# One order of the same operations exchanged for another: 2757 places, 425 PSUM banks and the engines of shared operations

## The chip, the core and the metric

The kernel runs on one core of a Trainium2 chip. The core has five instruction streams: TensorE (PE, with its weight loads PEld), VectorE (DVE), ScalarE (ACT), GpSimd (POOL) and SyncE (SP), which here only issues DMAs. Each works through its own list in order, and they meet through semaphores. The metric is device time in microseconds of one execution.

## The reference, cut to what matters

```python
# attention: batch 8, heads 8, seq 576, head_dim 64; block-causal mask, blocks of 64
scores = np.where(mask, scale * np.matmul(q, k.transpose(0, 1, 3, 2)), -1e9)
attn = np.exp(scores - np.max(scores, axis=-1, keepdims=True))
attn = attn / (np.sum(attn, axis=-1, keepdims=True) + 1e-09)
x = np.matmul(attn, v)            # then (8, 576, 512): heads side by side
# mixer, for each of the 8 batches
theta = x @ w_theta
zr, zi = x * np.cos(theta), x * np.sin(theta)
y = np.einsum('ts,bsd->btd', w_tok_r, zr) + np.einsum('ts,bsd->btd', w_tok_i, zi)
u = x + y
return u + np.maximum(u @ w_ch, 0.0)
```

All inputs and outputs are float32.

## The kernel before, in words

There are 64 heads (8 batches of 8). They go in 32 pairs; pair p works on heads 2p and 2p+1, and heads 8b to 8b+7 belong to batch b. A pair's scores are made on PE (L600, L612, with mask rows at L605), their row maxima on DVE (L630, L638), and the exponentials on ACT (L642) into the tiles `t`. The first four pairs turn these on PE (L654) and copy them out (L661, L663). All later ones split `t` into a high and a low float16 part `p` (high on ACT or DVE, L327 or L331; low on DVE, L669), and SP turns the parts with transposing DMAs into `pt`. PE multiplies `pt` with the parts of v (L689, "weighted"), DVE normalises into `x_ring` (L699 to L709), and POOL moves a 64-row piece (L715).

The mixer of batch b needs all its eight heads. `x_ring` is split into high and low parts `xp` (high on ACT or DVE, L325 or L331; low on DVE or POOL, L775), turned by DMA into `xt`; PE makes theta (L789); ACT and DVE make the fraction of a turn (L799, L805) and ACT the sines (L823, L825); the products with x (L835) and their high and low parts `zh` (L325, L329, L331) and `zl` (L848) are shared between DVE, POOL and ACT. PE sums over the sequence ("mix", L858). `u` starts as the sum of the parts of x (L863, DVE or POOL), is scaled (L327, L329, L331), takes the mix (L871), is split into `uhl` (L327 or L331, and L882), multiplied with w_ch on PE (L891), rectified and added (L897), scaled ("fin", L327, L329 or L331) and stored.

The weights are split in the same way at the start: L416 (ACT), L423 and L425 (DVE), L429 (ACT), and L436 (DVE) for the low parts such as `wch_l`.

Nothing sets the order but tables. The function `order_of` (L221) sorts the 2757 steps by the numbers in `PLACES`; each step emits its instructions in that order, so `PLACES` sets the order on every engine and on SP's queue. `BANKS` names the PSUM bank of each accumulation in turn. `ON` names, for each kind of shared operation, the engine of each instance: D for DVE, A for ACT, P for POOL. `RUNNING` (L192) lists fill matmuls, read at L1108 to L1114: an entry (n, bank, count) puts `count` matmuls of a tile of ones, whose result nobody reads, ahead of step n.

Of the kernel before, what the change touches and what calls it, by code (L numbers as in the profile page):

```python
# [189 lines left out]


RUNNING = [  # L192
    (8, 0, 3), (13, 4, 4), (37, 7, 23), (53, 2, 5), (359, 5, 5)
]
ON = {"w5": "DAADDADAD",
      "wc": "DDPPPPDDD",
      "vc": "PDDPDPPPPDPPDPPDDPPDDPPP",
      "qh": "PPPPPPPDPPAAPAADPAADAPADAAPADDAP",
      "vf": "PPDPPPPP",
      "cp": "DDDADAADAADDAAAAAAAAAAAAAAAAAAAA",  # L200
# [966 lines left out]
```

## Time and profile before

| what | us |
|---|---|
| median of 3 runs (661.02 to 663.47) | 663.03 |
| the profiled execution, its own time | 661.59 |
| its span in the profile | 659.8 |
| PE busy in the span | 643.2 |
| DVE busy | 580.5 |
| ACT busy | 466.7 |
| POOL busy | 328.2 |

The span runs from the first instruction to the last; 1.8 us of the execution's time lie around it. A PE matmul is pipelined: a row of 128x288 lasts 287 ns, but the next one starts 122 ns later, so a busy PE may still wait. To see who limits whom one asks, in each stretch, which engine has hardly any idle time, and how much work each engine has left.

### The profile page before, as it was taken

To read this page: it belongs to the slowest core of one execution; us is meant where nothing else is said; L and a number is where in the kernel's file an instruction comes from. 1 tells how busy PE (TensorE), PEld (TensorE's weight loads), DVE (VectorE), ACT (ScalarE), POOL (GpSimd) and SP (SyncE) were. 2 spreads that over 40 slices of the span, in tenths; PEclk is the share of its full clock that TensorE was granted. 3 is DMA by queue.
4 is the path that set the end of the run, shared out by engine and by line. 5 is a ranking of instruction groups with operands and counts; after the bars stand their busy time and mean duration, and the time that the engine had idled before them with its cause. 6 is when DMAs were issued, how large, how long until landed. Compare 5 with 4: busy or idle time off the path is not lost.

```text
span 659.8 us, 17344 instructions
## 1 busy us (share of the span) xinstructions
PE 643.2 (97%) x7153; PEld 504.0 (76%) x7153; DVE 580.5 (88%) x900; ACT 466.7 (71%) x719; POOL 328.2 (50%) x345
## 2 busy tenths in 40 slices
PE   8999989999999999999999999999999999999997
PEld 4899767887678767787787868887787867885775
DVE  4899999989999999999998998999879999754724
ACT  4997897775997788665984679678885887516411
POOL 2310357545528737585256466554574346552800
PEclk9999989999999999999999999999999999999999
DMA  8972288999999799699687879899678887740021
GB/s 308 352 254 77 47 205 145 201 221 180 229 199 182 175 190 192 144 202 177 158 201 187 150 177 183 185 210 240 120 175 160 139 192 131 113 114 19 1 90 73
DMA packets 247647, 110.51 MB, mean 167 GB/s; under 512 B 229008, under 2 KB 229008, under 8 KB 247568
## 3 DMA queue, kind: packets, MB, share of 16 engines
q1 hardware_dynamic: 247568, 109.41, 75.3%
q8 instruction: 56, 0.92, 0.6%
q14 instruction: 23, 0.19, 0.1%
HBM read 43.06 MB, written 9.44 MB: 80 GB/s over the span
## 4 chain that ended last, share of the span: by engine, by line
PE 68%; DVE 21%; ACT 5%; issue 4%; DMA 1%; POOL 0%; DVEq 0%; ACTq 0%; POOLq 0%
PE ps L858 25%; PE ps L891 10%; PE ps L689 10%; PE ps L789 10%; PE ps L600 9%; DVE m L638 5%; DVE p L669 3%; DVE v L586 2%; ACT t L642 1%; ACT p L327 1%; PE ps L654 1%; DVE zl L848 1%; PE ps L1113 1%; DVE u L897 1%; DVE wT_l L436 1%
## 5 line engine op out<-in xcount | busy, mean ns | idle before, releaser
L642 ACT ACTIVATE t<-ps,m 128x192 f32<-128x192 f32 (+4 forms) x288 | 140.8, 555 | 58.8 <-DVE m L638 40.2
L858 PE MATMUL ps<-wT_h,zl 128*128 128x288 f16 x540 | 155.0, 287 | 2.5 <-DVE zl L848 2.5
L858 PE MATMUL ps<-wT_h,zh 128*128 128x288 f16 x540 | 155.4, 288 | 0.7 <-ACT t L642 0.7
L858 PE MATMUL ps<-wT_l,zh 128*128 128x288 f16 x540 | 154.9, 287 | 0.0
L638 DVE TENSOR_REDUCE m<-ps 128x2 f32<-128x640 f32 (+3 forms) x128 | 117.4, 946 | 12.0 <-PE ps L605 11.5
L858 PEld LDWEIGHTS <-zh 128*128 128x128 f16 x1080 | 106.1, 98 | 27.8 <-issue 1.1
L689 PE MATMUL ps<-v,pt 128*128 128x65 f16 (+2 forms) x2668 | 113.3, 201 | 3.8 <-DVE x_ring L706 2.5
L669 DVE SCALAR_TENSOR_TENSOR p<-t,p 128x1664 f16<-128x1664 f32 x56 | 111.8, 2002 | 2.6 <-ACT p L327 2.5
L891 PE MATMUL ps<-uhl,wch_h 128*128 128x288 f16 x512 | 95.4, 286 | 1.1 <-DVE u L897 1.0
L689 PEld LDWEIGHTS <-pt 128*128 128x128 f16 x2436 | 81.5, 97 | 8.8 <-issue 5.5
L789 PE MATMUL ps<-wth_h,xt 128*128 128x512 f16 (+1 forms) x384 | 87.3, 345 | 0.3 <-DVE u L871 0.3
L789 PEld LDWEIGHTS <-xt 128*128 128x128 f16 (+1 forms) x576 | 46.4, 102 | 43.7 <-issue 2.4
L327 ACT ACTIVATE p<-t 128x1664 f16<-128x1664 f32 x46 | 73.3, 1599 | 3.7 <-DMA pt<-p 3.4
L891 PE MATMUL ps<-uhl,wch_l 128*128 128x288 f16 x256 | 73.2, 286 | 0.0
L858 PEld LDWEIGHTS <-zl 128*128 128x128 f16 x540 | 53.1, 98 | 16.3 <-DVE zl L848 3.2
L715 POOL COPY x_ring<-x_ring 64x64 f32<-64x64 f32 x64 | 37.9, 592 | 49.8 <-DVE x_ring L709 22.0
L891 PEld LDWEIGHTS <-wch_h 128*128 128x128 f16 x512 | 48.6, 98 | 14.8 <-issue 2.2
L789 PE MATMUL ps<-wth_l,xt 128*128 128x512 f16 (+1 forms) x192 | 57.3, 344 | 0.0
L835 POOL TENSOR_TENSOR aa<-aa,x_ring 128x512 f32<-128x512 f32 (+1 forms) x27 | 34.1, 1265 | 43.0 <-ACT aa L823 32.1
L775 POOL TENSOR_TENSOR xp<-x_ring,xp 128x640 f16<-128x640 f32 x17 | 28.6, 1682 | 34.2 <-ACT xp L325 21.3
L848 POOL TENSOR_TENSOR zl<-aa,zh 128x512 f16<-128x512 f32 (+1 forms) x27 | 33.7, 1252 | 16.4 <-ACT zh L325 12.9
L871 DVE SCALAR_TENSOR_TENSOR u<-ps,gain,u 128x288 f32<-128x288 f32 x64 | 31.2, 507 | 11.9 <-PE ps L858 11.9
(189 smaller groups left out, 1305.0 us busy)
## 6 DMA issues: line engine op xcount, KB each, us to landing
raw_v<-in_v SPq DMA_DIRECT2D x32, 384.0 KB, 4.7
q<-in_qT SPq DMA_DIRECT2D x32, 320.0 KB, 4.0
k<-in_kT SPq DMA_DIRECT2D x32, 320.0 KB, 4.0
out<-u SPq DMA_DIRECT2D x32, 288.0 KB, 3.1
w_raw<-in_w_tok SPq DMA_DIRECT2D x5, 576.0 KB, 4.4
p<-in_w_tok SPq DMA_DIRECT2D x4, 576.0 KB, 5.8
pt<-p SPq DMA_TRANSPOSE x112, 4.5
w_raw<-in_w_theta SPq DMA_DIRECT2D x2, 512.0 KB, 5.1
```

What stands on the lines that cost most here:

```text
L327: engine.mul(to, x, scale)
L600: nc.tensor.matmul(s[hh][:, col:col + n], lhsT=qq[rows, i * P:(i + 1) * P], rhs=kk[rows, k0:k0 + n], start=nn == 0 and (j == 0 or c == "ab ...
L638: nc.vector.tensor_reduce(out=m, in_=s, axis=AX.XY if i in (2, 3) else AX.X, op=ALU.max, negate=True)
L642: nc.scalar.activation(out=to, in_=s, func=AF.Exp, scale=1.0, bias=m)
L669: nc.vector.scalar_tensor_tensor(out=self.p[:, 1, :], in0=self.t, scalar=LIFT, in1=self.p[:, 0, :], op0=ALU.mult, op1=ALU.subtract)
L689: nc.tensor.matmul(to, lhsT=pp[:, block, :], rhs=x, start=nn == 0, stop=nn == n - 1)
L715: nc.gpsimd.tensor_copy(out=x[64 - 64 * hh:P - 64 * hh], in_=x[rows])
L789: nc.tensor.matmul(g[rows, 0:cols.stop - cols.start], lhsT=x[:, dt, part, i, rows], rhs=ww[:, dt, cols], start=(n == 0), stop=(n == 11))
L835: engine_of("z", (2 * self.b + hf) * 5 + n).tensor_tensor(out=cd, in0=cd, in1=x, op=ALU.mult)
L848: engine_of("zl", (2 * self.b + hf) * 5 + n).tensor_tensor(out=zl, in0=cv, in1=zh, op=ALU.subtract)
L858: nc.tensor.matmul(g, lhsT=zz[:, kk, cols], rhs=ww[:, kk, ts], start=(n == 0 and kk == k0 and nn == 0), stop=(n == 4 and nn == 2))
L891: nc.tensor.matmul(g[:, 0:HS], lhsT=ww[:, dt, e * P:(e + 1) * P], rhs=uu[:, dt, th * HS:(th + 1) * HS], start=(n == 0), stop=(n == 11))
```

## The change

The same steps are emitted with other tables. `PLACES` differs in 2632 of 2757 numbers and `BANKS` in 270 of 425. `RUNNING` goes from 40 fill matmuls in five places to 21 in three. In `ON` two kinds (`vf`, `cp`) stay as they are and in the others some instances change engine; as totals, DVE has 3 fewer `qh` (6 to 3), 5 fewer `xh` (18 to 13) and 5 fewer `fin` (16 to 11), and 3 more each of `z` (37 to 40) and `xs` (7 to 10), 2 more each of `xd` and `high`; ACT has 5 more `xh` and 5 more `fin`, POOL 3 fewer `xs` and 3 fewer `z`. No function is changed.

```diff
 PLACES = [
-    3, 2, 15, 19, 21, 62, 162, 197, 4, 5, 22, 30, 34, 65, 177, 191, 27, 26, 52, 61, 64, 92, 246, 255, 43, 40, 74,
+    2, 3, 15, 19, 22, 66, 142, 179, 4, 5, 23, 32, 35, 62, 157, 187, 26, 28, 54, 61, 65, 128, 257, 264, 40, 43, 72,
...
 RUNNING = [
-    (8, 0, 3), (13, 4, 4), (37, 7, 23), (53, 2, 5), (359, 5, 5)
+    (9, 0, 5), (33, 1, 13), (372, 0, 3)
 ]
...
-      "qh": "PPPPPPPDPPAAPAADPAADAPADAAPADDAP",
+      "qh": "APAPPPPAPAPAPDAADAPPAAPADAAPPPPA",
...
-      "xh": "AAAADADADDAAADDDADADDAADDAAADDAAAADDADD",
-      "xl": "DDDDDPPPPDDPDPDPDDDDDDPPDDPPPDPPPPDDDDP",
+      "xh": "AAAAAAAAADAAAADAAAADADDAADADDDAAAADDDAD",
+      "xl": "DDDDDPPPPDDPPPDPDDDDPPDPDDPPPDDPDPDPDDP",
...
-      "xs": "DDPDPPPDPPPDPPDD",
-      "xd": "AAPAAPAADDAAAPAP",
-      "uh": "AAAAADADAAAAADAA",
-      "fin": "PDAPDDDADDPPPADAADPAPADAAPPADDDDAPDPADDA"}
+      "xs": "DDPDPDDDPPDDDPPD",
+      "xd": "AAPAAAAADDPAPDDA",
+      "uh": "ADAAAAAAAAAAAADA",
+      "fin": "APADDDAPAPPAAPAAPDAADAPAADPADDDDAAAPPADP"}
```

The first rows of ACT in the program of before, at the start of the kernel (`w_raw` and `p` hold the first weight here, `t_94` and `t_95` are the exponentials of the first pair's two heads):

```order
L416 ACT_TABLE_LOAD
L416 ACTIVATE w_val<-w_raw 128x1024
L642 ACTIVATE t_95<-ps,m 128x64
L416 ACTIVATE w_val<-p 128x1024
L642 ACTIVATE t_95<-ps,m 128x576
L642 ACTIVATE t_94<-ps,m 128x576
L642 ACTIVATE t_94<-ps,m 128x448
L642 ACTIVATE t_95<-ps,m 128x448
```

and in the changed program:

```order
L549 ACT_TABLE_LOAD
L549 ACTIVATE qh<-q 128x640
L416 ACTIVATE w_val<-w_raw 128x1024
L642 ACTIVATE t_95<-ps,m 128x64
L416 ACTIVATE w_val<-p 128x1024
L642 ACTIVATE t_95<-ps,m 128x576
L642 ACTIVATE t_95<-ps,m 128x448
L642 ACTIVATE t_94<-ps,m 128x576
```

The first pair's `qh`, made by POOL before, is now ACT's first work, and the table load stands with it instead of with the first step on the weights; the exponentials follow in another order.

Rows of DVE in the program of before just ahead of the low part of head 32 (the first of batch 4), while batch 3 is in its mixer:

```order
L331 TENSOR_SCALAR zh<-rr 128x512
L699 TENSOR_SCALAR r<-ps 128x6
L706 TENSOR_TENSOR x_ring<-ps,r 128x4x64
L638 TENSOR_REDUCE m<-ps 128x2
L331 TENSOR_SCALAR xp<-x_ring 128x640
L775 TENSOR_TENSOR xp<-x_ring,xp 128x640
L701 RECIPROCAL r<-r 128x6
L709 TENSOR_SCALAR x_ring<-ps,r 64x64
L669 SCALAR_TENSOR_TENSOR p<-t_95,p 128x1664
L331 TENSOR_SCALAR u_75<-u_75,sizes 128x576
```

and those just ahead of the same head's low part in the changed program:

```order
L871 SCALAR_TENSOR_TENSOR u_74<-ps,gain,u_74 128x288
L699 TENSOR_SCALAR r<-ps 128x6
L701 RECIPROCAL r<-r 128x6
L669 SCALAR_TENSOR_TENSOR p<-t_94,p 128x1664
L565 SCALAR_TENSOR_TENSOR ql<-q,qh 128x640
L586 SCALAR_TENSOR_TENSOR v_86<-raw_v,sizes,v_86 128x12x64
L709 TENSOR_SCALAR x_ring<-ps,r 64x64
L706 TENSOR_TENSOR x_ring<-ps,r 128x5x64
L871 SCALAR_TENSOR_TENSOR u_74<-ps,gain,u_74 128x288 x3
L775 TENSOR_TENSOR xp<-x_ring,xp 128x640
```

Before, DVE makes both the high and the low part of one `xp` there (L331, L775) and scales a block of `u` (L331); in the changed program one low part of `xp` stands there, the high part and the scaled block are not in these rows, and the splits of q and v (L565, L586) have come in.

## Rows read from the trace of the kernel before

**Rows 1.** Stretches: length, busy us of PE, PEld, DVE, ACT, POOL; clock; DMA share

```profile
0.00:20.00 20.00, 16.90 (x86) 9.92 (x87) 10.59 (x14) 10.80 (x17) 3.58 (x24) 1.00 0.87 320
20.00:350.00 330.00, 322.50 (x3649) 255.94 (x3647) 319.46 (x500) 261.45 (x404) 169.53 (x177) 0.99 0.84 185
350.00:580.00 230.00, 228.04 (x2822) 181.55 (x2823) 211.38 (x321) 169.56 (x263) 126.89 (x118) 1.00 0.84 168
580.00:660.00 80.00, 75.74 (x603) 56.57 (x599) 39.11 (x69) 24.88 (x36) 28.22 (x28) 0.99 0.16 54
```

**Rows 2.** The page's chain of work that ended last, shares of the span

```profile
PE 68%; DVE 21%; ACT 5%; issue 4%; DMA 1%; POOL 0%; DVEq 0%; ACTq 0%; POOLq 0%
```

**Rows 3.** The same chain at the end, in time: start us, us, what

```profile
573.48 5.36 DMA pt<-p
...
580.51 13.23 PE ps L858 x108
593.75 11.90 PE ps L789 x72
605.64 11.88 PE ps L891 x96
617.52 26.46 PE ps L858 x216
643.98 11.77 PE ps L891 x96
```

**Rows 4.** The opening in time: start us, us, engine, operation [idle before <-releaser]

```profile
3.78 0.72 POOL L551 TENSOR_SCALAR qh<-q 128x640 f32<-128x640 f32 x1 [1.06 <-DMA q<-in_qT]
4.56 3.79 PE L600 MATMUL ps<-k,qh 64*128 64x288 f32 x16 [0.76 <-POOL qh L551]
8.01 1.28 ACT L416 ACT_TABLE_LOAD   x1 [8.01 <-DMA w_raw<-in_w_theta]
8.38 1.89 PE L1113 MATMUL ps<-ones 128*128 128x512 bf16 x4
8.49 1.36 DVE L638 TENSOR_REDUCE m<-ps 128x2 f32<-128x1152 f32 x1 [6.09 <-PE ps L605]
10.56 0.23 DVE L630 TENSOR_REDUCE m<-ps 128x1 f32<-128x64 f32 x1 [0.71 <-PE ps L612]
11.58 5.14 PE L1113 MATMUL ps<-ones 128*128 128x512 bf16 x23
17.70 1.96 DVE L663 TENSOR_SCALAR pt<-ps 128x1024 f32<-128x1024 f32 x2 [0.72 <-PE ps L654]
21.27 2.00 PE L600 MATMUL ps<-k,qh 64*128 64x288 f32 x16
```

**Rows 5.** ACT's first splits of q, as a group: busy us, mean ns | idle before

```profile
L549 ACT ACTIVATE qh<-q 128x640 f32<-128x640 f32 x2 | 1.5, 729 | 0.3 <-PE ps L605 0.3
```

**Rows 6.** DVE's groups of one shape: busy us, mean ns | idle before

```profile
L775 DVE TENSOR_TENSOR xp<-x_ring,xp 128x640 f16<-128x640 f32 x11 | 11.3, 1030 | 2.3 <-ACT xp L325 2.3
L863 DVE TENSOR_TENSOR u<-xt 128x1152 f32<-128x1152 f16 x7 | 9.9, 1417 | 7.7 <-DMA out<-u 7.7
L331 DVE TENSOR_SCALAR xp<-x_ring 128x640 f16<-128x640 f32 x11 | 6.1, 558 | 0.9 <-POOL x_ring L715 0.7
L331 DVE TENSOR_SCALAR u<-u,sizes 128x576 f32<-128x576 f32 x9 | 5.9, 660 | 0.0
L331 DVE TENSOR_SCALAR v<-raw_v,sizes 128x768 f16<-128x768 f32 x5 | 3.0, 610 | 0.0
```

**Rows 7.** POOL, then DVE, in time around 221 us

```profile
218.90 1.92 POOL L775 TENSOR_TENSOR xp<-x_ring,xp 128x640 f16<-128x640 f32 x1 [0.61 <-DVE xp L331]
220.77 2.38 POOL L863 TENSOR_TENSOR u<-xt 128x1152 f32<-128x1152 f16 x1
...
220.81 3.15 DVE L586 SCALAR_TENSOR_TENSOR v<-raw_v,sizes,v 128x768 f16<-128x768 f32 x1
```

**Rows 8.** All of line L586 on DVE: duration ns min/median/max

```profile
L586 DVE SCALAR_TENSOR_TENSOR v<-raw_v,sizes,v x28: 1001/1011/3152, 81.8 to 576.4; 128x768 f16<-128x768 f32 x28
```

More of the change, by code (lines that the diff above doesn't have):

```diff
@@ L32 @@
 PLACES = [
[142 rows of a table removed]
[142 rows of a table added]
 ]
 BANKS = [
[12 rows of a table removed]
[12 rows of a table added]
 ]
 RUNNING = [
-    (8, 0, 3), (13, 4, 4), (37, 7, 23), (53, 2, 5), (359, 5, 5)
+    (9, 0, 5), (33, 1, 13), (372, 0, 3)
 ]
-ON = {"w5": "DAADDADAD",
-      "wc": "DDPPPPDDD",
-      "vc": "PDDPDPPPPDPPDPPDDPPDDPPP",
-      "qh": "PPPPPPPDPPAAPAADPAADAPADAAPADDAP",
+ON = {"w5": "DDADDADAD",
+      "wc": "PDPPDDPPD",
+      "vc": "PDDPPDPDPDDPPPPDPDDDDDPP",
+      "qh": "APAPPPPAPAPAPDAADAPPAAPADAAPPPPA",
       "vf": "PPDPPPPP",
       "cp": "DDDADAADAADDAAAAAAAAAAAAAAAAAAAA",
-      "n0": "DAADDAADDDDAAADADADDADDADDDADDADDADDDADDDAAADADDADAAAADAAADADADD",
-      "v1": "DDDDPAPDPPPAADPAAAADADPAPPPAADPA",
-      "high": "DDDDDDDDAAAAAAAAAAAADAAADAAAAAADAADADAAADAAAAAADAAAAADAAADAADAAA",
-      "kh": "DDDDDDDDDDDDPAAAPAPAAADPPADAPAAA",
-      "kl": "DDDDDDDDDDDDDPPPDDDPDPDPDDDPPDDP",
-      "xh": "AAAADADADDAAADDDADADDAADDAAADDAAAADDADD",
-      "xl": "DDDDDPPPPDDPDPDPDDDDDDPPDDPPPDPPPPDDDDP",
-      "z": "DPPDDPPDDPPDDDPPPDPDDPPDPPPDPPDDPDDDPPPDPPPDPDPDDPPDDDPPDPDPDDDPPDPPPPPPPDPDDDPD",
-      "zh": "PAADPAPAAAPPDDPAAAAPPDDAAAAPDPPAPADAAPAPAADAAAPAAAADPPAAAAAAPPPADDADAPAAPAAADAAA",
-      "zl": "DPDDDPPPDPPPDDDDPDPDPPDDPDPPPPPPPDDPPPPPDPPPPDPPPDPPPDPPPPPDPDPPDPPPDDPDDDPPDPPP",
-      "xs": "DDPDPPPDPPPDPPDD",
-      "xd": "AAPAAPAADDAAAPAP",
-      "uh": "AAAAADADAAAAADAA",
-      "fin": "PDAPDDDADDPPPADAADPAPADAAPPADDDDAPDPADDA"}
+      "n0": "DAADDADDAADADDDADDDDADDADDADDDDDDADAAADAAAADAAAAAAADDADDDDAAADAD",
+      "v1": "DDDDPDPAAAPAPAAPAAPPAAPDDAPDAPPD",
+      "high": "DDDDDDDDAAAAAADAAAADDAAADAAAAAAADAAADADADAAADAAAAAAAAAAAADAADAAD",
+      "kh": "DDDDDDDDDDDDPAAAPPADAAPAPDPAPAPA",
+      "kl": "DDDDDDDDDDDDDPDDPDDPPDPDPPPPPDDP",
+      "xh": "AAAAAAAAADAAAADAAAADADDADAADDDAAAADDDAD",
+      "xl": "DDDDDPPPPDDPPPDPDDDDPPDPDDPPPDDPDPDPDDP",
+      "z": "DPPDPPPDDPDPPDPDDPPPPPPPPDDDDDPPPPDPDDDDPDDDDPPPDDDDPPDDPPDDPPDPPDPPPDDDDPDDDPDP",
+      "zh": "PADPAAAAPDPPAPAADAAADPADDPAPAADDAAAPAAAAAAPAPAAPPAAAADAPAADDAAPAAAPPDPAPAAAPAAAD",
+      "zl": "DDDPDPPDPPPPDDDPDPPDPPPPPPPPPDPDDDPPPPPPPDPDPDPPPDPDPPPDPPPPPDDDPPDDPPDDPPPPDDPP",
+      "xs": "DDPDPDDDPPDDDPPD",
+      "xd": "AAPAAAAADDPAPDDA",
+      "uh": "ADAAAAAAAAAAAADA",
+      "fin": "APADDDAPAPPAAPAAPDAADAPAADPADDDDAAAPPADP"}
 WHOLE = 4
```

306 rows, old and new, of tables (BANKS, PLACES) are left out of this document.

## The prediction

> **What bounds the kernel now.** I read the busy times by stretches first [rows 1]. From 20 to 350 us PE is busy 322.5 of 330 us and DVE 319.5, so two engines have next to nothing left, while ACT (261.5) and POOL (169.5) have room. From 350 to 580 us PE is busy 228.0 of 230 and DVE has 18.6 us idle: there PE alone limits. From 580 us on PE runs to its end and DVE is half idle. The first 20 us are different: DVE is busy 10.6 of 20. The chain of waits says the same: PE 68%, DVE 21%, ACT 5% [rows 2]. Its end is a run of PE work with nothing between: 13.23 + 11.90 + 11.88 + 26.46 + 11.77 = 75.2 us, begun once the last head's transposing DMA of 5.36 us had landed [rows 3].
>
> So I treat the kernel as DVE ahead and PE behind. At any point of the order, the time can't be less than the DVE work that stands ahead of it and the PE work that stands behind it. I took the mean cost of each instruction from its group (counting only up to the start of the next one, since DVE's instructions overlap: their durations sum to 639 us and DVE is busy 580.5) and summed along the order. PE's work without the fill matmuls is 618.6 us. In the order of before, DVE's work leads PE's by 11.1 us at head 12, 10.0 at head 20, 11.7 at head 28, 15.6 at head 36, and then by 12.8 at head 40 and 8.8 at head 52. The peak is 15.8, where batch 3 begins its mix. That gives 618.6 + 15.8 = 634.4 us. DVE's idle time is 9.4 us in the first 20 and 10.5 from 20 to 350; PE lacks 2.0 us from 350 to 580; from the end of the last PE run (643.98 + 11.77 = 655.75) to the end of the span are 4.05 us more. The sum is 660.4, against a span of 659.8. The account closes, and I use its terms for the change.
>
> **The change, part by part.**
>
> The sum of each engine's work hardly changes. With the same means DVE goes from 580.5 to 582.3 us, ACT from 466 to 468, POOL from 328 to 321, and PE loses 19 of 40 fill matmuls. At 5.14 us for 23 [rows 4] that is 0.22 us each, 4.2 us. I cost their removal at nothing: nearly all lie in the opening, where PE waits for DVE and ACT anyway. If PE were the limit there, the gain would be up to 4.2 us; I keep that for the lower end.
>
> The opening. Before, POOL makes the first `qh` when q has landed, at 3.78 us, in 0.72 us. ACT's table load of 1.28 us starts only at 8.01, since it waits with the first weight step for that weight's DMA [rows 4]. In the changed program ACT makes the first `qh`, and its table load stands first without a wait. ACT has nothing to do until 8.01, so the load is hidden before q lands. An ACT `qh` takes about what POOL takes (0.73 us, [rows 5]), so the scores start at the same time. What is won is the 1.28 us on ACT before the weight step. On DVE, two waits for PE may go: 0.71 us for the block of 64 columns (L630), which stands behind four fill matmuls of 1.89 us, and 0.72 us for the first turned exponentials (L663), which stand behind 23 more of 5.14 us [rows 4]. In the changed program there is no fill behind the first scores, and 13 instead of 23 before the turning. That is 1.4 us, on DVE, which is then full to 350 us. What could be late next is ACT's exponentials; they have the 1.28 us. Bounds: 0 to 2 us; I take 1.4.
>
> The middle. Between heads 12 and 40 the order and the engines change what DVE has to do: high parts of `xp` 7 to 2, low parts 7 to 5, `zl` from `aa` 5 to 2, `wch_l` 1 to 0 (moved ahead), scaled `u` blocks 6 to 3, high parts of v 3 to 0, but sums `u<-xt` 2 to 4 and high parts of p 6 to 7. The five kinds that change most in number or price are, by [rows 6], -5 x 0.56 - 2 x 1.03 - 3 x 0.66 - 3 x 0.61 + 2 x 1.42 = -5.8 us, -5.3 without the overlap; all the others, `wch_l`, `zl` and the parts of p among them, add -1.7, so -7.0. ACT takes 6.0 us more in that stretch, where it has some 20% idle. Ahead of head 12 DVE gets 2.2 us more (1.8 of it `wch_l`), and behind head 40, where PE limits, 3.7 more. The lead becomes 11.9 at head 12, 13.3 at 20, 12.4 at 28, 10.3 at 36, 8.0 at 40 and 4.8 at 52. The peak is now 14.6, in the mix of batch 1: a hill has been made a plateau. By peaks the gain is 1.3 us. Its bounds: if only the old hill counted, 15.6 - 10.3 = 5.3 us; if the plateau binds at each of its points and PE waits more often for it, a loss of 1 to 2.
>
> Behind the peak. From head 40 on DVE is 4 to 5 us earlier against PE than before. PE's missing 2.0 us from 350 to 580 [rows 1] are waits for such products; I take 1.6 of them (bounds 0 and 2.0).
>
> The end. Behind the last head stand 75.0 us of PE work by the means in both programs, and the last block is again rectified and scaled by DVE. The chains between the last mix and the last channel product differ, by 0.3 us at most: nothing.
>
> The port. A DVE split of v takes 1.01 us in the middle and 3.15 at most [rows 8]. The longest one started at 220.81, 0.04 us after POOL had begun a sum of 2.38 us, itself behind a POOL instruction that had just ended; DVE got its turn when POOL was done [rows 7]. Such long waits of DVE (0.9 us or more) are seven between 97 and 350 us, together some 9 us; [rows 7] show the longest. POOL's work in the middle is 135.6 us before and 134.4 after, so I see no fewer occasions and put nothing in the sum; the bounds are 4.5 us on either side (half of the seven gone, or half as many more).
> The Trainium skill (SBUF — State Buffer, section "Who interferes with whom") says that issue order, not the shape of the operation, decides who blocks. By that rule an order that lets POOL's long sums start first leaves DVE to pay each of them whole. The rows agree, and by it the sum could lose what a planner counts as won for POOL.
>
> Sum: -1.4 - 1.3 - 1.6 = -4.3 us: a span of 655.5 and, with 1.8 us around it, 657.3 against 661.6 of the profiled execution. The median of the runs is 1.4 above that execution, so I state 658.7.
>
> **The rivals.**
>
> *The plateau binds as the hill did.* From head 16 to head 32 the lead is up to 3.3 us higher than before, so PE waits for DVE earlier; the opening's 1.4 us may be eaten too if PE runs slow there. Of that the trace shows this: the first sixteen score matmuls took 3.79 us and later ones of the same kind 2.00 [rows 4]. The granted clock of the stretch reads 1.00 [rows 1] and so doesn't show it, but the pace is about that of the lower of the clock's two levels (1.2 against 2.4 GHz). Without fill behind them the next scores may still run at that pace, for about 1.3 us more. Then nothing is left but the 1.6: 661 to 664 against the median. In its favour: PE's and DVE's totals are the same.
> The Trainium skill (TensorE: Matmul & The Clock Gate, "What's actually happening") holds that the throttled level is the default and that activity releases it, which speaks against dropping fill; by it the sum would be -3.0.
>
> *The port gets better.* If half of DVE's long waits go, 4.5 us more come off: 654.2. For it speaks that POOL has fewer of its longest sums (`u<-xt`, 5 to 3 in the middle); against it that it gets more two-input work of other kinds there.
>
> *Slower: the port gets worse.* The place is the same stretch, heads 12 to 40. Every time POOL begins a long instruction just ahead of one of DVE's that needs the port, DVE loses 1.0 to 2.1 us. With three more of these the forecast is eaten; it is slower than before from the fourth on, and with six to seven more it stands at 667. For it: DVE now has four `u<-xt` instead of two there and POOL more `xp` and `zl`, all with two inputs. Against: it would need nearly twice as many as now.
>
> **How the numbers follow.** Forecast as summed, 658.7: 0.45. Plateau, 662.5: 0.27. Better port, 654.2: 0.12. Worse port, 667: 0.16. A measurement of this kernel can tell about 0.5% from no change, 3.3 us, so faster means below 659.7 and slower above 666.3. About a seventh of the forecast's share falls above 659.7: faster 0.50, same 0.35, slower 0.15. The range takes the better port with the fill gained (654.2 - 4.2 = 650) and the worse port: 650 to 667. Cases of one sign don't hold nearly all, so the forecast's own range: 655 to 662.
>
> **What would show it.** Right: the table load ahead of the first `qh`, the first L663 at about 16.3 instead of 17.7; DVE less busy from 250 to 350 us with PE still near full; PE not busy by under 1 us from 350 on; the run of 75 us at the end unchanged. Wrong: PE's gaps moved to heads 16 to 28 in full size; DVE's busy time over 585 us, or more splits of 2 to 3 us than the ones before, which would mean that the port decided; a first score block still waiting for the table load.

## The result, and the profile after

The kernel after takes 656.53 us (median of 16 runs, 654.66 to 662.52), the kernel before 662.89 us beside it (16 runs, 661.02 to 664.38). The ratio is 0.9914, 95% interval 0.9895 to 0.9933: 6.4 us less. I had said 658.7 us, 650 to 667. The profiled execution of after has a span of 654.7 us, 5.1 less than before's 659.8; I had said 655.5.

The page's span, the busy times of the engines and the shares of the chain of waits, the last to be read beside [rows 2]:

```profile
span 654.7 us, 17337 instructions
PE 635.9 (97%) x7134; PEld 500.7 (76%) x7134; DVE 574.3 (88%) x896; ACT 469.1 (72%) x727; POOL 310.5 (47%) x341
PE 78%; DVE 11%; DMA 4%; ACT 2%; issue 2%; POOL 2%; SPq 0%; DVEq 0%; POOLq 0%; ACTq 0%
```

The same stretches of after as in [rows 1] (length, busy us of PE, PEld, DVE, ACT, POOL; clock; DMA share; GB/s):

```profile
0.00:20.00 20.00, 13.94 (x78) 8.56 (x78) 11.05 (x14) 10.89 (x18) 3.06 (x23) 1.00 0.92 342
20.00:350.00 330.00, 322.29 (x3682) 257.61 (x3682) 317.36 (x496) 266.33 (x414) 156.76 (x175) 1.00 0.84 184
350.00:580.00 230.00, 229.09 (x2834) 182.14 (x2830) 212.76 (x328) 168.31 (x263) 128.60 (x120) 1.00 0.84 169
580.00:660.00 80.00, 70.62 (x551) 52.41 (x549) 33.14 (x61) 23.61 (x34) 22.09 (x24) 0.99 0.17 50
```

PE and DVE are still both full from 20 to 350 us, but more matmuls fit into those 330 us (3682, 3649 before). The chain moved from DVE (21% to 11%) to PE (68% to 78%). DVE is busy 574.3 us where I had summed 582.3, and POOL 310.5 where I had 321: both engines did less waiting inside their instructions than before. The end is the run of [rows 3], 75.2 us again. Here it is in time (start us, us, what):

```profile
575.43 13.23 PE ps L858 x108
588.66 11.90 PE ps L789 x72
600.55 11.76 PE ps L891 x96
612.32 26.46 PE ps L858 x216
638.77 11.86 PE ps L891 x96
```

**Where the time went.** To compare kernels at the same amount of work I summed PE's matmuls without the fill, each group at its mean cost, and read at what time each trace has reached the same sum. A point is named by its time in before. Against before, after is level at 77 us, 0.6 us ahead at 185, 0.9 at 227, 2.7 at 291, 4.1 at 373, 4.4 at 576, and 5.1 at the last matmul. So most of the gain comes between 185 and 373 us, and nothing in the opening.

For the same points I split DVE's time into idle time, the port excess (for each instruction, what it lasts beyond the shortest tenth of its shape) and the rest, its own work. The port excess of the whole run falls from 43 to 36 us. Its name stands for the inference that POOL holds these instructions up, and the traces bear it out: POOL is busy for half of the run, yet all but some 3 of the 43 us, and all but some 4 of the 36, belong to instructions of DVE beside which POOL was at work. The splits of v of [rows 8] and the low parts of p, all of L586 and then of L669 in after (duration ns min/median/max):

```profile
L586 DVE SCALAR_TENSOR_TENSOR v<-raw_v,sizes,v x28: 1001/1015/1473, 79.4 to 567.7; 128x768 f16<-128x768 f32 x28
L669 DVE SCALAR_TENSOR_TENSOR p<-t,p x56: 1872/1888/2856, 80.4 to 565.4; 128x1664 f16<-128x1664 f32 x56
```

No split of v is held for 2 us any more. [Rows 7] show why one did: POOL's sum of batch 2 began just ahead of it. In after the same sum stands beside DVE work on PSUM, which does not lengthen. POOL, then DVE, in time around it:

```profile
223.33 2.37 POOL L863 TENSOR_TENSOR u<-xt 128x1152 f32<-128x1152 f16 x1
...
223.81 1.36 DVE L871 SCALAR_TENSOR_TENSOR u<-ps,gain,u 128x288 f32<-128x288 f32 x3
225.09 1.08 DVE L638 TENSOR_REDUCE m<-ps 128x2 f32<-128x896 f32 x1
```

The opening of after, beside [rows 4]:

```profile
0.72 1.28 ACT L549 ACT_TABLE_LOAD   x1 [0.72 <-PEq L1152]
...
3.72 0.74 ACT L549 ACTIVATE qh<-q 128x640 f32<-128x640 f32 x1 [1.72 <-DMA q<-in_qT]
...
4.62 3.32 PE L600 MATMUL ps<-k,qh 64*128 64x288 f32 x16
...
9.42 2.98 PE L1113 MATMUL ps<-ones 128*128 128x512 bf16 x13
13.90 1.09 PE L654 MATMUL ps<-ident_r,t 128*128 128x128 f32 x8 [1.50 <-ACT t L642]
...
15.97 2.35 DVE L663 TENSOR_SCALAR pt<-ps 128x1024 f32<-128x1024 f32 x2
...
16.30 1.31 ACT L505 ACTIVATE unused<-raw_v 128x1280 uint8<-128x1280 f32 x1
...
19.13 0.15 DVE L509 TENSOR_REDUCE sizes<-sizes 128x1 f32<-128x2 f32 x1 [0.81 <-ACT unused L505]
...
19.82 0.22 PE L359 MATMUL ps<-unused,ones 128*128 128x128 bf16 x1 [1.12 <-POOL unused L353]
...
19.96 2.10 PE L600 MATMUL ps<-k,qh 64*128 64x288 f32 x16
...
22.20 2.89 POOL L580 TENSOR_SCALAR v<-raw_v,sizes 128x768 f32<-128x768 f32 x2 [1.36 <-DVE sizes L373]
...
24.25 3.00 PE L689 MATMUL ps<-v,pt 128*128 128x65 f32 x25 [1.16 <-POOL v L580]
```

Every step that I had forecast is there: the table load ahead of q, no wait of DVE's L663, which starts at 15.97 instead of 17.70. But head 0 (L689) starts at 24.25 us, and it started at 24.28 before. It waits for v, v for its scale, the scale for two sums over v on ACT (L505), and these stand behind the exponentials.

### The profile page after: what moved, and what is told of

The parts are those of the page before. It is cut to its first block, busy times and chain, and to the rows that moved or that the text cites. A ratio compares the mean times of both kernels' runs of the same rounds, so it can differ in the third digit from the quotient of the medians.

```text
span 654.7 us, 17337 instructions
## 1 busy us (share of the span) xinstructions
PE 635.9 (97%) x7134; PEld 500.7 (76%) x7134; DVE 574.3 (88%) x896; ACT 469.1 (72%) x727; POOL 310.5 (47%) x341
## 4 chain that ended last, share of the span: by engine, by line
PE 78%; DVE 11%; DMA 4%; ACT 2%; issue 2%; POOL 2%; SPq 0%; DVEq 0%; POOLq 0%; ACTq 0%
PE ps L858 30%; PE ps L789 12%; PE ps L891 12%; PE ps L689 12%; PE ps L600 10%; DVE m L638 3%; DVE p L669 1%; DMA w_raw<-in_w_theta 1%; DMA pt<-p 1%; DMA w_raw<-in_w_tok 1%; PE ps L612 1%; PE ps L654 1%; DVE wT_l L436 1%; DMA q<-in_qT 1%; DVE u L897 1%
## 5 line engine op out<-in xcount | busy, mean ns | idle before, releaser
L642 ACT ACTIVATE t<-ps,m 128x448 f32<-128x448 f32 (+4 forms) x288 | 142.1, 554 | 59.7 <-DVE m L638 32.4
L638 DVE TENSOR_REDUCE m<-ps 128x2 f32<-128x640 f32 (+3 forms) x128 | 117.2, 948 | 15.5 <-PE ps L605 14.3
L689 PE MATMUL ps<-v,pt 128*128 128x65 f16 (+2 forms) x2668 | 112.4, 201 | 4.3 <-DVE x_ring L706 1.9
L669 DVE SCALAR_TENSOR_TENSOR p<-t,p 128x1664 f16<-128x1664 f32 x56 | 112.6, 2013 | 0.7 <-ACT p L327 0.4
L689 PEld LDWEIGHTS <-pt 128*128 128x128 f16 x2436 | 80.6, 97 | 7.3 <-DMA pt<-p 3.0
L327 ACT ACTIVATE p<-t 128x1664 f16<-128x1664 f32 x44 | 70.0, 1595 | 0.6
L848 POOL TENSOR_TENSOR zl<-aa,zh 128x512 f16<-128x512 f32 (+1 forms) x30 | 36.6, 1219 | 27.9 <-ACT zh L325 14.6
L871 DVE SCALAR_TENSOR_TENSOR u<-ps,gain,u 128x288 f32<-128x288 f32 x64 | 31.2, 509 | 18.7 <-PE ps L858 18.4
L715 POOL COPY x_ring<-x_ring 64x64 f32<-64x64 f32 x64 | 31.0, 486 | 28.5 <-DVE x_ring L709 22.9
L327 ACT ACTIVATE uhl<-u,size_ch 128x1152 f16<-128x1152 f32 (+1 forms) x15 | 17.8, 1190 | 33.5 <-DVE u L871 33.3
L600 PE MATMUL ps<-kh,qh 64*128 64x288 f32 (+2 forms) x240 | 39.5, 312 | 1.1 <-POOL zh L329 0.5
```

The source lines that it names most:

```text
L327: engine.mul(to, x, scale)
L600: nc.tensor.matmul(s[hh][:, col:col + n], lhsT=qq[rows, i * P:(i + 1) * P], rhs=kk[rows, k0:k0 + n], start=nn == 0 and (j == 0 or c == "ab ...
L638: nc.vector.tensor_reduce(out=m, in_=s, axis=AX.XY if i in (2, 3) else AX.X, op=ALU.max, negate=True)
L642: nc.scalar.activation(out=to, in_=s, func=AF.Exp, scale=1.0, bias=m)
L669: nc.vector.scalar_tensor_tensor(out=self.p[:, 1, :], in0=self.t, scalar=LIFT, in1=self.p[:, 0, :], op0=ALU.mult, op1=ALU.subtract)
L689: nc.tensor.matmul(to, lhsT=pp[:, block, :], rhs=x, start=nn == 0, stop=nn == n - 1)
```

## The experiments

**Order and engines apart.** `engines_only` has the order, banks and fill of before and the engines of after; `order_only` is the reverse.

```diff
 ON = {
...
-      "xs": "DDPDPPPDPPPDPPDD",
+      "xs": "DDPDPDDDPPDDDPPD",
...
```

> The order, banks and fill of before, with the engines of the changed program. Theory A (the balance): the gain comes from DVE work that other engines take between heads 12 and 40, so that DVE's lead over PE falls; by the same sums as in the prediction the lead here is 13.6 at head 32, 10.1 at 36 and 8.5 at 40 (before 14.6, 15.6, 12.8), its peak 15.4 instead of 15.8. Expected by A: at least half of the 5.7 us, 657 to 660. Theory B (the port): the gain comes from an order that lets DVE stand less behind POOL; DVE's busy time stays at 580 or over and the time is that of before, 662 to 666, or more, since the old order was made for the old engines. Theory C (the fill): no change, 663.

> The order, banks and fill of the changed program, with the engines of before. Theory A: little is left, lead 13.2 at heads 32 and 36 and 11.8 at 40, peak 15.2; 661 to 664. Theory B: most of the 5.7 us stays, 657 to 659, with DVE's busy time some 5 us under that of before. Theory C (19 fewer fill matmuls are the gain): all of it stays, 656 to 658.

Measured: 705.77 us (ratio 1.0659, 1.0646 to 1.0673) and 694.60 us (1.0487, 1.0462 to 1.0511). No theory gave such times (for `engines_only` theory B's "or more" covers it in words alone). DVE's own work is that of before or after to within 2 us over the run, but waits appear on all engines. PE's waits in the profile of `engines_only` (engine, line, waited for: us in total, times, longest):

```profile
PE ps L891 <- DVE u L897: 7.2, 6, 2.9
PE ps L858 <- POOL zl L848: 4.1, 4, 1.9
PE ps L689 <- DVE x_ring L706: 3.7, 2, 2.8
```

At 576 us of before's time DVE has 29 us more idle time and 14 us more port excess there, `order_only` 20 and 13, gathered evenly from 80 us on. So this order and this assignment of engines belong together, and the two halves of the change can't be priced apart. They can be cut in time instead.

**The change cut in time.** At 170 us (after 721 steps) and at 358 us (after 1574) the two orders have done the same steps but for two or three. Each kernel below takes every stretch, with its order, banks and engines, from one of the two kernels. An example of the edit is `middle_part` against before:

```diff
 ON = {
...
-      "xh": "AAAADADADDAAADDDADADDAADDAAADDAAAADDADD",
+      "xh": "AAAADADADDAAAADAAAADADADDAAADDAAAADDADD",
-      "xs": "DDPDPPPDPPPDPPDD",
+      "xs": "DDPDPDDDPPPDPPDD",
...
```

> Steps 0 to 1573 in the order, on the banks and on the engines of the kernel after, the remaining 1183 in those of the kernel before. The two orders have done the same steps there but for three on each side. In the traces this cut lies at 358 us, where the kernel after is 4.1 us ahead. Theory A (the gain is made where it shows, and stays): the lead of 4.1 us is kept and the rest runs as before, so 658.5 us (657.5 to 659.5), with the lead at equal matmul work still 3.5 to 4.5 us at 540 us. Theory B (order and engines are one plan from end to end, so a cut costs, as the two mixed kernels showed): 663 us or more, with DVE's idle time behind the cut grown by over 2 us. Theory C (which instruction of DVE meets one of GpSimd at the port is dealt anew by every small shift): the lead at the cut is there, but the port excess of DVE behind the cut differs from that of before by over 2 us, and the end lies anywhere from 655 to 664.

> Steps 0 to 720 as in the kernel before (to 170 us), 721 to 1573 in the order, on the banks and on the engines of the kernel after (to 358 us), the rest as in the kernel before; at each cut two or three steps differ. Theory A: the opening and the first 170 us gave 0 to 0.6 us, the stretch from 170 to 358 us gave 3.5 to 4.1, so this stretch alone brings 659 us (658 to 660). Theory B (one plan): 663 us or more. Theory C: the stretch alone gives another gain than 3.5 to 4.1 us, between -2 and 6, because DVE comes into it at other moments than in the kernel after.

> Steps 0 to 1573 as in the kernel before (to 358 us), the rest in the order, on the banks and on the engines of the kernel after. Theory A: the last 300 us gave 1.0 to 1.2 us of the gain in the two traces, so 661.5 us (660.7 to 662.3), and the gains of this and of the first part add up to the whole. Theory B: 663 us or more. Theory C: 657 to 666 us, and the two gains do not add up.

> Steps 0 to 720 in the order, on the banks, on the engines and with the fill of the kernel after (to 170 us), the remaining 2036 as in the kernel before; two steps differ at the cut. Theory A (stretches add up: the first part measured 658.6 and the middle part alone 656.6, so the first 170 us of after cost 2.0 us): 664.6 us (663.8 to 665.4). Theory B (the trace of after, which stands level with before at 170 us): 662.3 us (661.5 to 663). Theory C (the port is dealt anew behind the cut): 660 to 667 us with the port excess of DVE between 170 and 358 us changed by over 2 us.

> Steps 0 to 720 as in the kernel before, with its fill (to 170 us), all others in the order, on the banks and on the engines of the kernel after. Theory A (the first 170 us of after cost 2 us and the last 300 give what they gave behind after's own middle, 658.6 to 656.5): 654.5 us (653.5 to 655.5), faster than both kernels. Theory B (the last part gives nothing unless DVE comes into it as in after; alone it gave 0): 656.6 us (655.8 to 657.4). Theory C: 653 to 660 us, with the port excess of DVE.

| kernel | to 170 us | 170 to 358 | from 358 | us | ratio to before, interval |
|---|---|---|---|---|---|
| `opening_part` | after | before | before | 663.32 | 1.0032 (1.0005 to 1.0060) |
| `middle_part` | before | after | before | 656.58 | 0.9904 (0.9890 to 0.9919) |
| `last_part` | before | before | after | 662.70 | 1.0006 (0.9996 to 1.0016) |
| `first_part` | after | after | before | 658.61 | 0.9945 (0.9924 to 0.9965) |
| `after_from_170` | before | after | after | 655.01 | 0.9880 (0.9862 to 0.9897) |

Before, beside them, took 662.6 us. The stretch from 170 to 358 us alone is worth 6.0 us, nearly the whole gain. The opening costs 0.8 by the medians (2.0 by `first_part` against `middle_part`). The last part gives nothing alone, but 1.6 behind the middle of after (655.0 against 656.6) and 2.1 behind its first part (656.5 against 658.6). Theory B (a cut costs) is out for `first_part` and `middle_part`. Theory A hits `first_part` and `after_from_170`, and the middle alone brings 2 us more than it said; it fails for the last part, which gives nothing unless the middle of after stands ahead of it. For `opening_part` no theory holds: 663.3 lies between those of A and B, and the port excess between 185 and 373 us (15.0 against 15.8) did not move by the 2 us of C. `after_from_170` beats before, and lies 1.5 us under after, though the two intervals still touch.

Where the last part loses can be seen in its trace: level with before at 373 us, it falls 2.4 us behind by 450, with a port excess of 7.8 us there against 3.4 in before and 5.9 in after, and wins 1.3 back by 540.

In the traces, between the points 185 and 373 us of before, DVE's time divides so:

| kernel | order there | us passed | own work | port excess | idle |
|---|---|---|---|---|---|
| before | before | 187.9 | 165.7 | 15.8 | 6.5 |
| `last_part` | before | 188.4 | 165.5 | 16.7 | 6.2 |
| `opening_part` | before | 188.1 | 166.2 | 15.0 | 6.9 |
| after | after | 184.4 | 161.2 | 14.5 | 8.5 |
| `first_part` | after | 183.6 | 162.3 | 13.2 | 8.1 |
| `middle_part` | after | 182.9 | 162.7 | 10.7 | 9.6 |
| `after_from_170` | after | 184.1 | 161.6 | 13.2 | 9.3 |

The order of after saves 3 to 5 us of DVE's own work there and 1 to 5 of port excess, and gives 2 to 3 back as idle time. With one and the same order the port excess goes from 10.7 to 14.5 us. How DVE comes in can be only a part of that: `middle_part` and `after_from_170` are the same program up to 358 us, and between 185 and 353 us their executions still differ by 1.5 us of port excess (10.2 and 11.7); after and `first_part`, likewise the same to there, by 0.5 (13.1 and 12.6). One profiled execution of each says no more.

**Two meetings taken away.** In before, the two sums of batch 2 on POOL are met by a split of v [rows 7] and by a low part of p.

```diff
         def add_parts(self, dp):
...
+            if self.b == 2:
+                return
             engine_of("xs", self.b * 2 + dp).tensor_tensor(out=self.u_two(dp), in0=high, in1=low, op=ALU.add)
```

> The kernel before without the two sums of the parts of x of batch 2 on GpSimd (L863, 2.38 us each, at 220.77 and 239.82 us); u of that batch then holds what was in the buffer before. In the trace of before these two are met by L586 (3.15 us in place of 1.00) and L669 (3.18 in place of 1.88), 3.4 us of DVE's time. Theory A (a meeting at the port costs the end what it costs DVE): the port excess of DVE falls by 3.4 us by 291 us, the time at equal matmul work is 2.5 to 3.4 us less there, and the end comes at 659.5 us (658.5 to 660.5). Theory B (a meeting that is taken away comes back with the next instruction of GpSimd, which now starts 2.4 us earlier, or DVE idles instead): under 1 us less, 661.7 to 663. Theory C (the port is bookkeeping and DVE is not what limits there): no change at 291 us, 662.6 us.

Measured: 660.12 us, ratio 0.9958 (0.9942 to 0.9974), 2.4 us less, as theory A said. In before the second sum and the low part beside it stand so (POOL, then DVE):

```profile
239.82 2.37 POOL L863 TENSOR_TENSOR u<-xt 128x1152 f32<-128x1152 f16 x1
...
240.76 3.18 DVE L669 SCALAR_TENSOR_TENSOR p<-t,p 128x1664 f16<-128x1664 f32 x1
```

The same split of v and the same low part of p, on DVE in the trace of `two_sums_out`:

```profile
221.53 1.01 DVE L586 SCALAR_TENSOR_TENSOR v<-raw_v,sizes,v 128x768 f16<-128x768 f32 x1
...
240.00 1.89 DVE L669 SCALAR_TENSOR_TENSOR p<-t,p 128x1664 f16<-128x1664 f32 x1
```

The split takes 1.01 us instead of 3.15, the low part 1.89 instead of 3.18. Of the 3.4 us, the port excess between 185 and 373 us keeps 2.6 as a gain (15.8 to 13.2); the other 0.8 is no more than two executions of one program differ by. The time in that stretch fell by 2.3 us (187.9 to 185.6) and the end by 2.4, while DVE's idle time there stayed at 6.6 us (6.5 before): no wait of DVE went with the sums. So what DVE loses at the port in this stretch, the kernel loses. POOL also has 4.8 us less to do here; that this wins nothing by itself is argued, from POOL being idle for half of the run, and not shown.

**One kind put back.** `sums_back` is after with the engines of before for the sums (`xs`): POOL 9 of 16 instead of 6.

```diff
-      "xs": "DDPDPDDDPPDDDPPD",
+      "xs": "DDPDPPPDPPPDPPDD",
```

> The changed program with one kind of operation, the sums of x's parts (L863, 128x1152), on the engines of before: three more of sixteen on POOL, three fewer on DVE. By the means DVE has 4.0 us less work and POOL 9.2 more; the peak of the lead stays at 14.6, behind head 24 it is 1.5 to 4 us lower. Theory A: the same or up to 2 us faster than the changed program, 654.5 to 657. Theory B: slower, since DVE pays up to 2.4 us whenever one of POOL's sums starts ahead of it; 658 to 662.

Measured: 657.68 us, ratio to before 0.9945 (0.9925 to 0.9964), against 0.9914 (0.9895 to 0.9933) for after; the intervals overlap, and the time lies between theory A (up to 657) and theory B (658 or more). By 576 us of before's time DVE's own work is 4.9 us less than in after and its port excess 5.0 more: what the move to POOL saves on DVE it pays back at the port. The port excess by then is that of before again (39 us in both, 34 in after).

**The fill.** `less_fill` is before with 21 fill matmuls instead of 40, `more_fill` is after with 38 instead of 21.

```diff
-    (8, 0, 3), (13, 4, 4), (37, 7, 23), (53, 2, 5), (359, 5, 5)
+    (8, 0, 3), (37, 7, 13), (359, 5, 5)
```

```diff
-    (9, 0, 5), (33, 1, 13), (372, 0, 3)
+    (9, 0, 5), (33, 1, 20), (56, 0, 5), (74, 0, 5), (372, 0, 3)
```

> Before, with 21 instead of 40 fill matmuls: those between the first two blocks of scores and those at the second turning gone, 13 instead of 23 ahead of the first turning. Theories A and B: no change, 663 within 1.5, though the first copy of turned exponentials (L663) starts up to 1.4 us earlier. Theory C: 4.2 us less, 659.

> The kernel after with 38 fill matmuls in place of 21 (before has 40): 7 more ahead of the first turn, 5 ahead of the matmul that waits for the scale of v, 5 ahead of head 0, where PE waits 1.50, 1.12 and 1.16 us in the trace of after. Theory A (the fill keeps TensorE's clock up in the opening and does nothing else): no execution with a mean granted clock under 0.996, none over 658.5 us (two of 16 executions of after had 0.985 and 0.990 and took 662.5 and 662.2), and the median 656.5 us, within 0.7. Theory B (fill is dead weight that pushes real matmuls back): median 657 to 658.5 us. Theory C (what sets the clock of the slower executions lies elsewhere than in the opening): median as in A, but again executions under 0.992 and over 661 us.

Measured: `less_fill` 665.41 us, ratio 1.0049 (1.0031 to 1.0066), so taking fill away gains nothing and costs a little: theory C is out, and A and B missed by 0.9 us. In its trace 0.2 us are lost by 227 us and 4.0 by 556, with the port excess 4.4 us up. The stretch from 20 to 24 us, in `less_fill` and then in before (columns as in [rows 1]):

```profile
20.00:24.00 4.00, 4.00 (x22) 3.08 (x24) 2.69 (x4) 2.84 (x6) 3.05 (x3) 0.57 0.77 273
...
20.00:24.00 4.00, 3.83 (x35) 3.12 (x35) 3.88 (x7) 3.50 (x6) 2.59 (x3) 1.00 0.82 320
```

Only the fill differs, and the granted clock is 0.57 instead of 1.00 there. The two of its six executions with a mean granted clock of 0.998 or more took 663.4 and 663.7 us, the four with 0.993 to 0.996 took 665.0 to 666.8. How a short fall of the clock at 20 us comes to cost most at 540 to 556 us is open.

`more_fill` took 655.96 us, 0.9901 (0.9883 to 0.9918): as fast as after, by the intervals, with no execution over 657.85, as theory A said. Fill is no dead weight.

What can happen with little fill was seen in `opening_part`, whose profiled execution took 670.48 us. Its stretches (columns as in [rows 1]):

```profile
9.00:13.00 4.00, 2.58 (x12) 0.98 (x10) 2.90 (x4) 2.78 (x4) 0.00 (x0) 1.00 1.03 415
13.00:17.00 4.00, 2.68 (x16) 2.15 (x16) 3.96 (x5) 4.00 (x9) 0.72 (x1) 0.84 1.03 406
17.00:20.00 3.00, 2.83 (x15) 2.43 (x14) 2.23 (x4) 2.10 (x5) 0.40 (x1) 0.64 1.03 413
20.00:24.00 4.00, 3.04 (x28) 2.62 (x28) 3.25 (x6) 4.00 (x7) 2.07 (x2) 1.00 0.73 284
24.00:28.00 4.00, 3.81 (x26) 3.81 (x26) 4.00 (x8) 3.26 (x6) 1.42 (x3) 0.75 0.85 306
28.00:32.00 4.00, 4.00 (x21) 4.00 (x20) 2.28 (x4) 3.57 (x7) 0.00 (x0) 0.50 1.04 412
32.00:36.00 4.00, 4.00 (x21) 4.00 (x20) 2.99 (x4) 0.00 (x0) 1.33 (x1) 0.50 0.58 232
```

and PE around the first turns there (start us, us, what, idle before and its releaser):

```profile
8.60 2.98 PE L1113 MATMUL ps<-ones 128*128 128x512 bf16 x13
13.84 1.09 PE L654 MATMUL ps<-ident_r,t 128*128 128x128 f32 x8 [2.26 <-ACT t L642]
15.41 1.70 PE L654 MATMUL ps<-ident_r,t 128*128 128x128 f32 x8 [0.48 <-ACT t L642]
```

The 13 fill matmuls end at 11.58 us, and PE idles 2.26 us for ACT's exponentials. Eight turns then take 1.09 us, the next eight 1.70. The granted clock falls to 0.64, recovers, and stands at 0.50, the lower of its two levels, from 28 to 36 us. At 77 us this execution is 6.1 us behind before, at the end 8.6. The profiled execution of after has the same 13 fill matmuls and 1.50 us of idle PE at the same place, and its clock kept 1.00. Before fills that gap with 23 matmuls, which end at 16.7 us [rows 4]. Over the runs, leaving out `less_fill` and the two mixed kernels: with after's opening and its 21 fill matmuls (after, `first_part`, `opening_part`, `scale_first`, `sums_back`) 7 of 52 executions had a mean granted clock of 0.990 or less, and each took 4.7 to 7.2 us more than its kernel's median. With the opening of before and its 40 (51 executions of before, and 27 of `middle_part`, `last_part`, `after_from_170`, `two_sums_out`) none was under 0.994. The six of `more_fill` were at 0.997 or more; six are too few to show that the 17 fill matmuls alone do it. The two openings differ in order and engines too, so the 7 of 52 are put down to the fill by argument; `less_fill`, the one run in which only the fill of before's opening changes, shows the fall of the clock but had no execution under 0.993. Fill in the opening is no safeguard for what comes later: `engines_only`, with before's 40, had 0.989 to 0.990, its clock falling from 90 us on.

**The scale first.** `scale_first` is after with the two sums over v (L505) ahead of the last two exponentials of head 0.

```diff
 PLACES = [
-    2, 3, 15, 19, 22, 66, 142, 179, 4, 5, 23, 32, 35, 62, 157, 187, 26, 28, 54, 61, 65, 128, 257, 264, 40, 43, 72,
+    2, 3, 15, 19, 22, 66, 142, 179, 4, 5, 23, 32, 35, 62, 157, 187, 26, 28, 54, 61, 65, 128, 257, 264, 42, 45, 72,
...
```

> The kernel after with one thing moved: the two sums over v of batch 0 on ACT (L505), from which the scale of v follows, stand ahead of the last two exponentials of head 0 instead of behind them; two of PE's turns of the first pair come later by the 2.9 us of the two sums. In the trace of after head 0 starts at 24.25 us because it waits for v (L580 at 22.20), which waits for the scale, which waits for these sums (16.30 to 19.10). Theory A (that chain sets the start of head 0, and the opening sets the end): the sums start 0.8 to 1.4 us earlier, head 0 starts at 23.2 us (22.8 to 23.6), and the end comes 0.8 to 1.2 us earlier, at 655.5 us. Theory B (head 0 comes earlier, but DVE's own list, which is full from there on, sets the rest): head 0 at 23.2 us, no lead left at 100 us, and the end at 656.5 us, within 1 us. Theory C (the shift deals the meetings at the port anew): the end moves by 1 to 4 us to either side, with the port excess of DVE, and not with head 0.

Measured: 655.85 us, ratio 0.9897 (0.9880 to 0.9913): against after's 0.9914 (0.9895 to 0.9933) no difference is shown. In its trace:

```profile
15.88 1.31 ACT L505 ACTIVATE unused<-raw_v 128x1280 uint8<-128x1280 f32 x1
...
19.94 0.82 DVE L663 TENSOR_SCALAR pt<-ps 128x640 f32<-128x640 f32 x1 [1.08 <-PE ps L654]
20.69 0.28 DVE L366 TENSOR_REDUCE sizes<-ps 128x1 f32<-128x128 f32 x1
...
22.49 2.89 POOL L580 TENSOR_SCALAR v<-raw_v,sizes 128x768 f32<-128x768 f32 x2 [1.06 <-DVE sizes L373]
```

The sums start 0.42 us earlier, not 0.8 to 1.4, and the scale is no earlier: its next step on DVE (L366) stands behind a copy of turned exponentials (L663), which now waits 1.08 us for the turn that the sums pushed back. v is made at 22.49 us instead of 22.20, and head 0 at 25.24, since PE ran at a granted clock of 0.57 from 20 to 24 us in this execution. So theories A and B missed their head 0 of 23.2 us, and C its 1 to 4 us at the end; that the end lies where A and B had it tells nothing between them. In the opening several chains of waits run side by side, and loosening one tightened the next.

## Why the prediction was right, point by point

The total came out (-4.3 forecast, -5.1 in the traces, -6.4 by the medians), but three of its terms were wrong, and they cancelled in part. That DVE's time in the middle decides was right; that the sum came so close was in part luck. Two sums of the working do not come out either. DVE's changes of +2.2, -7.0 and +3.7 us add to -1.1, where the totals said +1.8. And PE's 618.6 us without fill are not what means of the trace give: PE is busy 643.2 us and its 40 fill matmuls are 9 to 11 of that, so some 633 are left. The closing of the account of before can't be followed from the trace.

**The opening, -1.4: wrong, 0 in the trace.** The two waits of DVE went and L663 came 1.7 us earlier, as said, and by 77 us DVE has idled 1.0 us less than in before. Two steps let that be lost. One is "what could be late next is ACT's exponentials; they have the 1.28 us": behind these exponentials stood the sums over v and with them the scale and head 0, which I had not followed. The other is DVE's own work, 0.9 us more by 77 us and 2.3 more by 185; I had seen it coming (2.2 ahead of head 12), but took it only into the lead, away from the peak. Which of the two weighs more is not shown, since `scale_first` did not bring head 0 forward. The opening as a whole costs 0.8 us by the median of `opening_part`.

**The middle, -1.3: right in kind, too small.** DVE's own work in the stretch fell by 3.0 to 4.5 us and the time by 3.5 to 5.0. I had the 7.0 us less for DVE between heads 12 and 40, and then let only the highest point of DVE's lead over PE count, 15.8 to 14.6. But DVE idles 6.5 of 188 us there: it is the limit over the whole length, not at the top of the hill, and work saved anywhere in the stretch came through, less 1.6 to 3.1 us of new idle time. My bound for that case, 5.3, was the better value. The plateau rival is seen only in that idle time.

**The port, 0: wrong, and the largest error in DVE's time.** After pays 3.3 us less at the port by 353 us and 4.7 by 576. Up to 373 us, where DVE is nearly full, its 4.1 us are made up of some 2.9 less at the port (1.7 of it before 185 us, where the added own work eats it), 2.2 less own work and 1.1 more idle time; what the port gives later, where PE limits, brings next to nothing. I had compared POOL's work (135.6 and 134.4 us) and concluded that there were no fewer occasions. What counts is what stands beside POOL's long instructions: two sums of before cost DVE 3.4 us, the same sums in after, one of them now DVE's own work, nearly nothing at the port, and `two_sums_out` prices the two at 2.4 us of the end. The better-port rival had named `u<-xt` on POOL (5 to 3 in the middle) and got 0.12. `sums_back` bears out that cause, and shows its price: the port excess saved is bought with 4.9 us of DVE's own work. The rival's own condition did not come true, though: of the long waits (0.9 us or more, 97 to 350 us) there are seven in after too, 7.3 us together against some 9. The Trainium skill (SBUF — State Buffer, section "Who interferes with whom") has issue order decide who blocks; the rows agree, 3.15 us beside a sum that began 0.04 us earlier and 1.01 without it.

**Behind the peak, -1.6: about the size, but not for the reason.** The trace gives -1.0, the medians 1.6 to 2.1, yet `last_part` alone gives 0. PE's missing time did fall, from 1.96 to 0.91 us between 350 and 580. Alone, the last part loses 2.4 us between 373 and 450 us, with 4.4 us more port excess; why that does not happen behind the new middle is open.

**The fill, at nothing: right for the median, probably wrong for the spread.** `less_fill` and `more_fill` show no gain from leaving it out. I had weighed it as PE time; in the trace of `less_fill`, with less of it, the granted clock falls from 20 to 24 us. 7 of 52 executions with after's opening paid 4.7 to 7.2 us, and the missing fill is the likely but not the shown cause. My rival had seen the first scores at the lower pace, but expected 1.3 us at most.

**The end, unchanged: right**, 75.2 us in both.

## What to carry to other kernels

Where an engine is busy all along a stretch, count its work over the whole stretch, and not only the highest point of its lead. Before moving work to an engine that can hold another up, as POOL held DVE here, look at what will run beside each long instruction: the sum of work told nothing about the meetings here. And an order with its engines is one plan: it can be cut at a moment where both plans have done the same steps, and there the pieces can be measured and put together (655.01 us here, better than before and at least as good as after), but exchanging one half of its tables cost 4.9 and 6.6%.

## What the runs showed of the hardware that I had not expected

- The same order paid 10.7 to 14.5 us of port excess in the same stretch, and kernels that are the same program up to 358 us differed by up to 1.5 us between 185 and 353. Taking 19 fill matmuls out of the opening of before cost 3 us, in its trace nearly all of it some 500 us later, with the port excess.
- A POOL instruction with two inputs from SBUF did not lengthen DVE's work on PSUM (L638 1.08 us beside a sum of 2.37; over all of after the 32 of this shape took 1.05 to 1.08, the 64 of L871 0.48 to 0.52), but held a split of 1.01 us until it took 3.15.
- After 2.26 us of idle PE behind the fill, the granted clock fell, and it stayed at 0.50 from 28 to 36 us although PE was busy 4.00 of 4.00 us in both windows. The Trainium skill (TensorE: Matmul & The Clock Gate, "What's actually happening") calls the throttled level the default and says activity releases it. By that rule the fall behind idle time is no surprise, and the trace agrees; the level of 0.50 in two windows in which PE never paused is what the rows add.
- The page's clock can read 1.00 while the first 16 score matmuls take 3.32 us (2.10 for 16 of them at 19.96 us in after).
